# Two decode attentions on one core: B's output weights in other pieces, the last buffers in the free K slot, two result rows

## The chip, the cores and the metric

One core of a Trainium2 chip runs the whole program. The time is the device time of one execution in microseconds (us). Before the change it is 825.41 us, the median of three runs (825.28 to 825.46).

## What is computed

Two attentions, A and B, each of one new token with 32 heads of 128 numbers over a cache of 16384 positions. A uses the whole cache, B only the last 4096 positions. Both results, 512 numbers each, stand side by side in the output.

```
q = x @ wq                                  # [1,512] @ [512,4096], as 32 heads of 128
scores = einsum("bhqd,bhkd->bhqk", q, k) * Dh**-0.5
o = einsum("bhqk,bhkd->bhqd", softmax(scores), v)
out = o.reshape(1, 1, 4096) @ wo            # [1,4096] @ [4096,512]
a: k, v = the whole cache;  b: k, v = cache[:, :, Sk - 4096:, :]
return concatenate([a, b], axis=-1)
```

All inputs are bf16. The caches that are read make 335 MB (268 for A, 67 for B), the four weight matrices 17 MB. Each number of the caches is used once.

## The kernel before

**Tiling.** The work goes in 20 steps (`steps`, `NT`): 16 of A with two heads each, 4 of B with eight heads each; the steps 0, 7, 13 and 19 are B's. Each step has one K tile and one V tile of 8 MB, 128 partitions of 64 KB. K tiles rotate through two slots (`kring`), V tiles through one (`vring`). The weights pass through the V slot too: `wq` of both sides at the start, `wo` of both at the end; the last V tile (`vlast`) goes into a K slot.

**A step.** VectorE multiplies K by q in halves (`scores_prod`, L206) and adds up over the 128 numbers of a head by halving (`scores_tree`, L212, L216). The maximum of each partition (L224) is transposed on TensorE (L228) into a PSUM bank from the pool `ps_m`, taken by head (L234), spread (L238) and transposed back (L241). ScalarE makes the exponentials (L253) and sets them into a masked weight tile `pm` (L260). TensorE multiplies with V (`pv`, L272): 64 matmuls in four column groups of 32 columns each, which write the four quarters of a PSUM bank. `fold` copies that bank to SBUF (`osb`, one buffer with the tag `o4`, L285) and adds the quarters by an fp32 matmul into the side's accumulator (L288).

**The end.** After the last step's maximum (`tile_max`), `normalize`, `own_o` and `spread_o` turn a side's accumulator into `Op`, 128x32 in bf16, one column per row block r of `wo` (L306 to L327). `wo` lies in SBUF as 128 partitions by 32 rows of 512: "row" below is this r, 1 KB per partition, 128 KB in all. A's projection (`project_a`, L336) takes the 32 rows of A in four column groups with 512 columns each, ScalarE copies the result (L341), and a matmul adds the four quarters (`finish_a`, L346). B's projection (`project_b`, L357) cuts every row in four quarters of 128 columns, one per column group; the result stands in four partitions, is cast (L362) and leaves by four output transfers (L364), two from SyncE's queue and two from ScalarE's.

**What sets the order.** The instructions of each engine are in the order of the code (`manual_schedule`). All large loads are issued by SyncE (SP) in order and wait there for a free slot; the 16 DMA engines work their share of each transfer in order of issue. Each load also adds to one of eight counters when it lands. The counters are used in turn, and a load waits until the one before it on its counter has landed. B's `wo` comes in pieces of 16, 8, 4, 3 and 1 rows (`wo_pieces`, `load_wo`, L143) and TensorE waits for each piece where it first reads it.

Of the kernel before, what the change touches and what calls it, by code (L numbers as in the profile page):

```python
# [9 lines left out]
F32 = mybir.dt.float32  # L10
BF16 = mybir.dt.bfloat16
P = 128
# [4 lines left out]
HQ, DH = 32, 128  # L17
# [8 lines left out]
def kernel(  # L26
# [14 lines left out]
    nc = tc.nc  # L41
# [4 lines left out]
    DN = A_wo.shape[1]  # L46
# [5 lines left out]
    kring = ctx.enter_context(tc.tile_pool(name="kring", bufs=2))  # L52
    vring = ctx.enter_context(tc.tile_pool(name="vring", bufs=1))
    small = ctx.enter_context(tc.tile_pool(name="small", bufs=3))
    one = ctx.enter_context(tc.tile_pool(name="one", bufs=1))
    ps_t = ctx.enter_context(tc.tile_pool(name="ps_t", bufs=2, space=bass.MemoryType.PSUM))
    ps_o = ctx.enter_context(tc.tile_pool(name="ps_o", bufs=1, space=bass.MemoryType.PSUM))
    ps_m = ctx.enter_context(tc.tile_pool(name="ps_m", bufs=2, space=bass.MemoryType.PSUM))

    NG = 4  # L60
    QR = P // NG
# [9 lines left out]
    ones = singles.tile([P, 1], F32, tag="ones")  # L71
    fours = singles.tile([P, P], F32, tag="fours")
# [3 lines left out]
    for k, (s, n, x, wq, wo, nh) in enumerate(((A, "A", A_x, A_wq, A_wo, 2), (B, "B", B_x, B_wq, B_wo, 4))):  # L76
# [8 lines left out]
        s.mask = singles.tile([P, nh], F32, tag=f"mask{n}", name=f"mask{n}")  # L85
        s.acc = ps_o.tile([P, 512], F32, tag=f"acc{n}", name=f"acc{n}")
    o_banks = [ps_o.tile([P, 512], F32, tag=f"o{k}", name=f"o{k}") for k in range(2)]

    def by_head(s, ap):
        if s is A:  # L90
# [11 lines left out]
    NT = len(steps)  # L102
# [36 lines left out]
    def load_wo(s, pieces):  # L139
        src = s.wo.rearrange("(p r) f -> p r f", r=HQ)  # L140
        r = 0
        for n in pieces:
            nc.sync.dma_start(out=s.wo_t[:, r : r + n, :], in_=src[:, r : r + n, :])  # L143
            r += n

    def make_masks(s):
# [73 lines left out]
    def tile_max(T):  # L220
        un = tiles[T]
        U = un.s.units
        m = small.tile([P, 2], F32, tag="m", name="m")
        nc.vector.tensor_reduce(  # L224
            out=m[:, 0:U], in_=un.sc[:, :].rearrange("p (u n) -> p u n", u=U), axis=AX.X, op=ALU.max
        )
        un.sm = ps_m.tile([P, P + 2], F32, tag="sm", name="sm")
        nc.tensor.transpose(un.sm[0:U, 0:P], m[:, 0:U], identf[:, :])  # L228

    def max_all(T):  # L230
        un = tiles[T]
        s, U = un.s, un.s.units
        M = small.tile([2, 4], F32, tag="M", name="M")
        nc.vector.tensor_reduce(  # L234
            out=M[0:U, 0 : s.nh], in_=by_head(s, un.sm[0:U, 0:P]), axis=AX.X, op=ALU.max
        )
        Mr = one.tile([2, P], F32, tag="Mr", name="Mr")
        nc.vector.tensor_copy(  # L238
            by_head(s, Mr[0:U, :]), M[0:U, 0 : s.nh].unsqueeze(2).broadcast_to([U, s.nh, P // s.nh])
        )  # L240
        nc.tensor.transpose(un.sm[:, P : P + U], Mr[0:U, :], identf[0:U, 0:U])  # L241
# [38 lines left out]
    def fold(T, u):  # L280
        un = tiles[T]
        s = un.s
        rows = 4 * s.nh
        osb = one.tile([P, 512], F32, tag="o4", name="o4")
        nc.scalar.copy(osb[:, :], un.o[u][:, :])  # L285
        per = QR // rows
        q, off = divmod(s.units * un.g + u, per)
        nc.tensor.matmul(  # L288
            s.acc[QR * q : QR * (q + 1), :], lhsT=s.fold[:, (per - 1 - off) * rows : (per - 1 - off) * rows + QR],
            rhs=osb[:, :], start=(off == 0), stop=(off == per - 1),  # L290
        )

    def square():
        return one.tile([P, P], F32, tag="sq", name="sq")

    def pick_blocks(o, src, n, weight):
        nc.vector.tensor_scalar(out=o, in0=src[:, 0:n], scalar1=weight[:, 0:1], scalar2=None, op0=ALU.mult)
        for j in range(1, 4):
            nc.vector.scalar_tensor_tensor(
                out=o, in0=src[:, j * n : (j + 1) * n], scalar=weight[:, j : j + 1], in1=o, op0=ALU.mult, op1=ALU.add  # L300
            )

    def normalize(s):
        n = HQ // s.nh
        sums = square()
        nc.vector.tensor_tensor(  # L306
            out=sums[:, :].rearrange("p (t h c) -> p t h c", t=n, h=s.nh),
            in0=s.cs[:, :].unsqueeze(2).unsqueeze(3).broadcast_to([P, n, s.nh, 4]),
            in1=s.mask[:, :].unsqueeze(1).unsqueeze(3).broadcast_to([P, n, s.nh, 4]), op=ALU.mult,
        )  # L310
        s.ps = ps_t.tile([P, 1 + P], F32, tag="tp", name="sums")
        nc.tensor.matmul(s.ps[:, 0:1], lhsT=sums[:, :], rhs=ones[:, :], start=True, stop=True)
        s.rq = small.tile([P, 5], F32, tag="rq", name="rq")
        nc.vector.reciprocal(s.rq[:, 4:5], s.ps[:, 0:1])
        nc.vector.tensor_scalar(
            out=s.rq[:, 0:4], in0=quad[:, :], scalar1=s.rq[:, 4:5], scalar2=None, op0=ALU.mult
        )

    def own_o(s):
        s.own = square()  # L320
        pick_blocks(s.own[:, :], s.acc[:, :], DH, quad)

    def spread_o(s):
        nc.tensor.matmul(s.ps[:, 1 : 1 + P], lhsT=fours[:, :], rhs=s.own[:, :], start=True, stop=True)
        t = small.tile([P, HQ], F32, tag="t", name="t", bufs=1)
        pick_blocks(t[:, :], s.ps[:, 1 : 1 + P], HQ, s.rq)
        nc.vector.tensor_copy(s.Op[:, :], t[:, :])  # L327

    def o_column(s, r):
        return s.Op[:, r : r + 1].broadcast_to([P, QR])  # L330

    def project_a():
        ps = ps_t.tile([P, DN], F32, tag="tp", name="wide")
        for r in range(HQ):
            g = r % NG
            nc.tensor.matmul(  # L336
                ps[QR * g : QR * (g + 1), :], lhsT=o_column(A, r), rhs=A.wo_t[:, r, :],
                start=(r < NG), stop=(r >= HQ - NG),
            )
        A.wide = one.tile([P, DN], F32, tag="o4", name="wide_sb")  # L340
        nc.scalar.copy(A.wide[:, :], ps[:, :])  # L341

    def finish_a():
        ps = ps_m.tile([1, DN], F32, tag="sm", name="out_a")
        first = A.fold[:, QR - A.rows : QR - A.rows + 1]
        nc.tensor.matmul(ps[:, :], lhsT=first, rhs=A.wide[:, :], start=True, stop=True)  # L346
        row = one.tile([1, DN], BF16, tag="sc", name="row_a")
        nc.scalar.copy(row[:, :], ps[:, :])
        for f in range(0, DN, DN // 2):
            nc.scalar.dma_start(out=out[0, :, f : f + DN // 2], in_=row[:, f : f + DN // 2])  # L350

    def project_b():
        w = DN // NG
        ps = ps_m.tile([P, w], F32, tag="sm", name="out_b")
        for r in range(HQ):
            for g in range(NG):
                nc.tensor.matmul(  # L357
                    ps[QR * g : QR * (g + 1), :], lhsT=o_column(B, r), rhs=B.wo_t[:, r, g * w : (g + 1) * w],
                    start=(r == 0), stop=(r == HQ - 1),
                )  # L360
        rows = one.tile([P, w], BF16, tag="Mr", name="rows_b")
        nc.vector.tensor_copy(rows[:, :], ps[:, :])  # L362
        for g in range(NG):
            (nc.sync if g % 2 else nc.scalar).dma_start(  # L364
                out=out[0, :, DN + g * w : DN + (g + 1) * w], in_=rows[QR * g : QR * g + 1, :]
            )

    wo_pieces = (16, 8, 4, 3, 1)
    with tc.manual_schedule():
        xrow = one.tile([2, D], BF16, tag="pm", name="xrow")  # L370
        for s in (B, A):
# [36 lines left out]
        for T in range(NT):  # L408
            if T >= 1:
                if T + 1 < NT:  # L410
                    new_k(T + 1)
                    load_k(T + 1)
                else:
                    load_v(T, kslot("vlast"))
            scores_prod(T, 0)
            if T >= 1:
                max_all(T - 1)
                soft(T - 1)
            scores_tree(T, 0)
            if T >= 1:  # L420
                for u in range(tiles[T - 1].s.units):
                    pv(T - 1, u)
                for u in range(tiles[T - 1].s.units):
                    fold(T - 1, u)
            if T + 1 < NT:
                load_v(T, vslot("vt"))
            else:
                wot = vslot("wot")
                for k, s in enumerate((A, B)):
                    s.wo_t = flat(wot[:, k * CH : (k + 1) * CH, :]).rearrange("p (r f) -> p r f", r=HQ)  # L430
                load_wo(A, (HQ,))
                load_wo(B, wo_pieces)
            scores_prod(T, 1)
            scores_tree(T, 1)
            tile_max(T)
        max_all(NT - 1)
        soft(NT - 1)
        normalize(A)
# [1 line left out]
        pv(NT - 1, 0)  # L440
        spread_o(A)
        pv(NT - 1, 1)
        for u in range(2):
            fold(NT - 1, u)
        normalize(B)
        own_o(B)
        project_a()
        spread_o(B)
        finish_a()
        project_b()  # L450


# [28 lines left out]
```

## Time and profile before

| | us |
|---|---|
| median of three runs | 825.41 |
| the profiled execution | 825.65 |
| its span, first to last instruction | 823.9 |
| VectorE busy | 766.4 (93%) |
| TensorE matmuls busy | 184.5 (22%) |
| ScalarE busy | 61.4 (7%) |
| `vlast` issued | 761.25 |
| `wo` of A issued, then B's pieces | 786.96 |
| last piece of B's `wo` issued | 801.1 |
| `OpA` ready | 808.99 |
| first output transfers (A) issued | 817.22 |
| B's cast (L362) begins | 821.14 |

The profile is one execution. The page lists each engine's busy time, a line of digits for 40 slices of the span (9 is a share of 90% or more), and the chain of work that ended last: from the last instruction back, at each step, to what released it. A window gives the busy time in one stretch; its DMA share is the mean over the 16 DMA engines, so 0.25 means four engines' worth of work. The timeline merges like instructions that follow each other, and names in square brackets the idle time ahead of them and what ended it. "SPq" and "ACTq" are the issuing of transfers by SyncE and ScalarE. The trace also records each addition to a counter by a landing transfer; these are called completion records here.

### The profile page before, as it was taken

The numbers are of one execution on the slowest core, as the hardware profiler recorded it, in microseconds if no ns is written. First come the engines' busy times: TensorE is split into PE (matmuls) and PEld (weight loads), VectorE is DVE, ScalarE is ACT, GpSimd is POOL, SyncE is SP. The second block draws the span as 40 slices with busy tenths as digits, with TensorE's granted clock in tenths as the row PEclk, the third lists the DMA queues.
The fourth block names the chain that finished last, engine by engine and source line by source line (L and its number), as shares of the span: only waits on it lengthen the run. The fifth ranks groups of instructions, "written<-read, shape, count | busy, mean of one in ns | idle before, by whom it ended". The sixth has DMA issues, their size and how long they took to land.

```text
span 823.9 us, 3928 instructions
## 1 busy us (share of the span) xinstructions
PE 184.5 (22%) x1606; PEld 60.9 (7%) x1606; DVE 766.4 (93%) x348; ACT 61.4 (7%) x165; POOL 0.7 (0%) x6
## 2 busy tenths in 40 slices
PE   3402312213030303220303112030402030303037
PEld 1100000001010001000000001010100010101012
DVE  2899899999999999999999999999999998999992
ACT  0102000001010000100000001010200000000011
POOL 0000000000000000000000000000000000000000
PEclk9755556565665656555656565555656565656568
DMA  9999999999999999999999999999999999999997
GB/s 384 434 431 435 449 420 449 426 437 433 430 436 430 422 441 439 414 449 427 439 423 443 420 445 413 453 417 428 435 449 420 452 418 442 427 422 441 423 429 292
DMA packets 8097, 352.57 MB, mean 428 GB/s; under 512 B 908, under 2 KB 1040, under 8 KB 1296
## 3 DMA queue, kind: packets, MB, share of 16 engines
q1 hardware_dynamic: 8068, 352.33, 99.2%
q8 instruction: 12, 0.20, 0.1%
q14 instruction: 5, 0.04, 0.0%
q10 hardware_dynamic: 12, 0.00, 0.0%
HBM read 352.32 MB, written 0.00 MB: 428 GB/s over the span
## 4 chain that ended last, share of the span: by engine, by line
DMA 56%; DVE 43%; issue 0%; SPq 0%; PE 0%; DVEq 0%
DMA kt<-in_A_k_cache_dram 44%; DVE kt L206 20%; DVE kt L212 20%; DMA kt<-in_B_k_cache_dram 5%; DMA vlast<-in_B_v_cache_dram 4%; DMA wot<-in_B_wo_dram 4%; DVE sc L216 3%; DVE Mr L238 0%; DVE M L234 0%; SPq L135 0%; SPq L122 0%; PE out_b L357 0%; DVE rows_b L362 0%; DVEq L216 0%
## 5 line engine op out<-in xcount | busy, mean ns | idle before, releaser
L212 DVE TENSOR_TENSOR kt<-kt 128x8192 bf16<-128x8192 bf16 (+3 forms) x160 | 345.0, 2156 | 4.8
L206 DVE TENSOR_TENSOR kt<-kt,qA 128x16384 bf16<-128x16384 bf16 x32 | 278.0, 8687 | 13.2 <-DMA kt<-in_A_k_cache_dram 13.2
L272 PE MATMUL o<-vt,pm 128*8 128x512 bf16 (+1 forms) x1216 | 113.9, 553 | 181.7 <-DMA vt<-in_A_v_cache_dram 161.1
L206 DVE TENSOR_TENSOR kt<-kt,qB 128x16384 bf16<-128x16384 bf16 x8 | 69.5, 8684 | 14.1 <-DMA kt<-in_B_k_cache_dram 14.1
L228 PE MATMUL sm<-identf,m 128*1 128x128 f32 (+1 forms) x20 | 7.4, 371 | 235.2 <-DVE m L224 235.2
L272 PEld LDWEIGHTS <-pm 128*8 128x8 bf16 (+1 forms) x1280 | 39.9, 114 | 253.2 <-issue 206.8
L216 DVE TENSOR_REDUCE sc<-kt 128x128 f32<-128x1024 bf16 x40 | 48.8, 1220 | 2.7
L241 PE MATMUL sm<-identf,Mr 1*128 1x1 f32 (+1 forms) x20 | 5.2, 261 | 178.5 <-DVE Mr L238 178.5
L247 ACT ACTIVATE bias<-sm 128x1 f32<-128x1 f32 (+1 forms) x20 | 3.4, 172 | 447.3 <-PE sm L241 447.3
L285 ACT COPY o<-o 128x512 f32<-128x512 f32 x24 | 14.1, 587 | 264.6 <-PE o L272 233.8
L228 PEld LDWEIGHTS sm<-identf,m 128*1 128x1 f32 (+1 forms) x20 | 1.6, 79 | 252.4 <-issue 241.2
L288 PE MATMUL accA<-o,foldA 128*32 128x512 f32 x32 | 16.7, 605 | 11.1 <-ACT o L285 11.1
L241 PEld LDWEIGHTS sm<-identf,Mr 1*128 1x128 f32 (+1 forms) x20 | 3.5, 176 | 184.9 <-DVE Mr L238 184.9
L260 ACT ACTIVATE pm<-p,maskA 128x256 bf16<-128x256 bf16 x32 | 14.5, 502 | 0.5
L183 PE MATMUL qp<-wqt,xbA 128*128 128x512 bf16 x32 | 9.4, 465 | 10.6 <-DMA wqt<-in_A_wq_dram 10.6
L253 ACT ACTIVATE p<-sc,bias 128x256 bf16<-128x256 f32 (+1 forms) x24 | 11.3, 472 | 0.6
L288 PE MATMUL accB<-o,foldB 128*32 128x512 f32 x16 | 9.9, 709 | 2.7 <-ACT o L285 2.7
L260 ACT ACTIVATE pm<-p,maskB 128x128 bf16<-128x128 bf16 x32 | 10.3, 392 | 0.3
L183 PE MATMUL qp<-wqt,scratch 128*128 128x512 bf16 x32 | 8.9, 447 | 5.0 <-DMA wqt<-in_B_wq_dram 5.0
L224 DVE TENSOR_REDUCE m<-sc 128x1 f32<-128x256 f32 (+1 forms) x20 | 8.4, 420 | 0.7
L272 PE MATMUL o<-vlast,pm 128*16 128x512 bf16 x64 | 6.1, 552 | 1.6 <-ACT pm L260 1.6
L234 DVE TENSOR_REDUCE M<-sm 1x2 f32<-1x128 f32 (+1 forms) x20 | 5.4, 271 | 0.6 <-PE sm L228 0.6
(60 smaller groups left out, 52.9 us busy)
## 6 DMA issues: line engine op xcount, KB each, us to landing
kt<-in_B_k_cache_dram SPq DMA_DIRECT2D x8, 4096.0 KB, 30.0
vt<-in_B_v_cache_dram SPq DMA_DIRECT2D x6, 4096.0 KB
vlast<-in_B_v_cache_dram SPq DMA_DIRECT2D x2, 4096.0 KB, 39.2
wqt<-in_B_wq_dram SPq DMA_DIRECT2D x1, 4096.0 KB, 12.5
wqt<-in_A_wq_dram SPq DMA_DIRECT2D x1, 4096.0 KB
wot<-in_A_wo_dram SPq DMA_DIRECT2D x1, 4096.0 KB
wot<-in_B_wo_dram SPq DMA_DIRECT2D x1, 2048.0 KB
wot<-in_B_wo_dram SPq DMA_DIRECT2D x1, 1024.0 KB
```

The lines of the kernel that those rows point to most:

```text
L183: nc.tensor.matmul(qp[:, :, :], lhsT=s.xb[:, j, c, :], rhs=wq[:, c, j, g : g + 4, :], start=(k == 0), stop=(k == n - 1),)
L206: nc.vector.tensor_tensor(out=k, in0=k, in1=s.q[:, j : j + 1, :].broadcast_to([P, CH, DH]), op=ALU.mult)
L212: nc.vector.tensor_tensor(out=k[:, :, 0:w], in0=k[:, :, 0:w], in1=k[:, :, w : 2 * w], op=ALU.add)
L216: nc.vector.tensor_reduce(out=tiles[T].sc[:, u * CH : (u + 1) * CH], in_=k[:, :, 0:8], axis=AX.X, op=ALU.add)
L224: nc.vector.tensor_reduce(out=m[:, 0:U], in_=un.sc[:, :].rearrange("p (u n) -> p u n", u=U), axis=AX.X, op=ALU.max)
L228: nc.tensor.transpose(un.sm[0:U, 0:P], m[:, 0:U], identf[:, :])
L241: nc.tensor.transpose(un.sm[:, P : P + U], Mr[0:U, :], identf[0:U, 0:U])
L253: nc.scalar.activation(out=un.part(p, u), in_=un.part(un.sc, u), func=ACT.Exp, scale=inv, bias=bias[:, u : u + 1], accum_out=s.cs[:, col + ...
L260: nc.scalar.activation(out=un.pm[u][:, :, j, :], in_=un.part(p, u).rearrange("p (i c) -> p i c", c=4), func=ACT.Copy, scale=s.mask[:, j : ...
L272: nc.tensor.matmul(o[r0 : r0 + rows, :], lhsT=un.pm[u][:, i, :, :].rearrange("p a b -> p (a b)"), rhs=V[T][:, u * un.n + 4 * i : u * un.n ...
L285: nc.scalar.copy(osb[:, :], un.o[u][:, :])
L288: nc.tensor.matmul(s.acc[QR * q : QR * (q + 1), :], lhsT=s.fold[:, (per - 1 - off) * rows : (per - 1 - off) * rows + QR], rhs=osb[:, :], s ...
```

## The change

B's pieces become 8, 8, 3, 8, 4 and 1 rows, and the piece of three rows is split by partitions into 119 and 9. B's first 19 rows are multiplied whole, with 512 columns in four column groups as A's are, copied by VectorE into `s.wide`, and added to the result by a join of two fp32 matmuls (`join_b`). The rows 19 to 31 are cut in two halves of 256 columns and use two column groups. B's result stands in two partitions and leaves by two output transfers, one per queue. The tile `late` (8 buffers of 512 fp32 numbers) takes the K slot that the last K tile leaves: the two last folds, the wide copies of A and B, and the squares of `normalize` and `own_o` have a buffer each, where one `o4` and one `sq` were shared. `normalize(B)` moves ahead of the last folds. Two fixed PSUM banks (`sm_banks`) take the place of the pool `ps_m`.

```diff
-    ps_m = ctx.enter_context(tc.tile_pool(name="ps_m", bufs=2, space=bass.MemoryType.PSUM))
+    sm_banks = [ps_o.tile([P, 512], F32, tag=f"sm{k}", name=f"sm{k}") for k in range(2)]
...
-        for n in pieces:
-            nc.sync.dma_start(out=s.wo_t[:, r : r + n, :], in_=src[:, r : r + n, :])
+        for n, cuts in pieces:
+            for a, b in zip((0,) + cuts, cuts + (P,)):
+                nc.sync.dma_start(out=s.wo_t[a:b, r : r + n, :], in_=src[a:b, r : r + n, :])
             r += n
...
-        un.sm = ps_m.tile([P, P + 2], F32, tag="sm", name="sm")
+        un.sm = sm_banks[T % 2]
...
-        osb = one.tile([P, 512], F32, tag="o4", name="o4")
+        osb = late[:, u, :] if T == NT - 1 else one.tile([P, 512], F32, tag="o4", name="o4")
...
-        sums = square()
+        sums = late[:, 4 + s.k, 0:P]
...
-        s.own = square()
-        pick_blocks(s.own[:, :], s.acc[:, :], DH, quad)
+        s.own = late[:, 6 + s.k, 0:DH]
+        pick_blocks(s.own, s.acc[:, :], DH, quad)
...
-    def project_a():
+    def wide_rows(s, n):
         ps = ps_t.tile([P, DN], F32, tag="tp", name="wide")
-        for r in range(HQ):
+        for r in range(n):
             g = r % NG
             nc.tensor.matmul(
-                ps[QR * g : QR * (g + 1), :], lhsT=o_column(A, r), rhs=A.wo_t[:, r, :],
-                start=(r < NG), stop=(r >= HQ - NG),
+                ps[QR * g : QR * (g + 1), :], lhsT=o_column(s, r), rhs=s.wo_t[:, r, :],
+                start=(r < NG), stop=(r >= n - NG),
             )
-        A.wide = one.tile([P, DN], F32, tag="o4", name="wide_sb")
-        nc.scalar.copy(A.wide[:, :], ps[:, :])
+        s.wide = late[:, 2 + s.k, :]
+        if s is A:
+            nc.scalar.copy(s.wide, ps[:, :])
+        else:
+            nc.vector.tensor_copy(s.wide, ps[:, :])
...
-    def project_b():
-        w = DN // NG
-        ps = ps_m.tile([P, w], F32, tag="sm", name="out_b")
-        for r in range(HQ):
-            for g in range(NG):
+    def tail_b(r0, r1, wide):
+        w = DN // 2
+        for r in range(r0, r1):
+            for g in range(2):
                 nc.tensor.matmul(
-                    ps[QR * g : QR * (g + 1), :], lhsT=o_column(B, r), rhs=B.wo_t[:, r, g * w : (g + 1) * w],
-                    start=(r == 0), stop=(r == HQ - 1),
+                    sm_banks[1][QR * g : QR * (g + 1), 0:w], lhsT=o_column(B, r),
+                    rhs=B.wo_t[:, r, g * w : (g + 1) * w], start=(r == wide), stop=(r == HQ - 1),
                 )
+    def join_b():
+        w = DN // 2
+        for g in range(2):
+            nc.tensor.matmul(
+                sm_banks[1][QR * g : QR * (g + 1), 0:w], lhsT=first.broadcast_to([P, QR]),
+                rhs=B.wide[:, g * w : (g + 1) * w], start=False, stop=False,
+            )
+    def store_b():
+        w = DN // 2
+        rows = one.tile([2 * QR, w], BF16, tag="Mr", name="rows_b")
+        nc.vector.tensor_copy(rows[:, :], sm_banks[1][0 : 2 * QR, 0:w])
+        for g, queue in enumerate((nc.sync, nc.scalar)):
+            queue.dma_start(out=out[0, :, DN + g * w : DN + (g + 1) * w], in_=rows[QR * g : QR * g + 1, :])
...
-    wo_pieces = (16, 8, 4, 3, 1)
+    wo_pieces = ((8, ()), (8, ()), (3, (119,)), (8, ()), (4, ()), (1, ()))
+    wide_n = 19
...
+        late = kring.tile([P, 8, 512], F32, tag="kring", name="late")
         max_all(NT - 1)
         soft(NT - 1)
         normalize(A)
...
         pv(NT - 1, 1)
+        normalize(B)
         for u in range(2):
             fold(NT - 1, u)
-        normalize(B)
         own_o(B)
-        project_a()
+        wide_rows(A, HQ)
         spread_o(B)
         finish_a()
-        project_b()
+        wide_rows(B, wide_n)
+        tail_b(wide_n, 27, wide_n)
+        join_b()
+        tail_b(27, HQ, wide_n)
+        store_b()
```

More of the change, by code (lines that the diff above doesn't have):

```diff
@@ L291, in fold @@
         )
-    def square():
-        return one.tile([P, P], F32, tag="sq", name="sq")
     def pick_blocks(o, src, n, weight):
@@ L304, in normalize @@
         n = HQ // s.nh
-        sums = square()
+        sums = late[:, 4 + s.k, 0:P]
         nc.vector.tensor_tensor(
-            out=sums[:, :].rearrange("p (t h c) -> p t h c", t=n, h=s.nh),
+            out=sums.rearrange("p (t h c) -> p t h c", t=n, h=s.nh),
             in0=s.cs[:, :].unsqueeze(2).unsqueeze(3).broadcast_to([P, n, s.nh, 4]),
@@ L311, in normalize @@
         s.ps = ps_t.tile([P, 1 + P], F32, tag="tp", name="sums")
-        nc.tensor.matmul(s.ps[:, 0:1], lhsT=sums[:, :], rhs=ones[:, :], start=True, stop=True)
+        nc.tensor.matmul(s.ps[:, 0:1], lhsT=sums, rhs=ones[:, :], start=True, stop=True)
         s.rq = small.tile([P, 5], F32, tag="rq", name="rq")
@@ L319, in own_o @@
     def own_o(s):
-        s.own = square()
-        pick_blocks(s.own[:, :], s.acc[:, :], DH, quad)
+        s.own = late[:, 6 + s.k, 0:DH]
+        pick_blocks(s.own, s.acc[:, :], DH, quad)
     def spread_o(s):
-        nc.tensor.matmul(s.ps[:, 1 : 1 + P], lhsT=fours[:, :], rhs=s.own[:, :], start=True, stop=True)
+        nc.tensor.matmul(s.ps[:, 1 : 1 + P], lhsT=fours[:, :], rhs=s.own, start=True, stop=True)
         t = small.tile([P, HQ], F32, tag="t", name="t", bufs=1)
@@ L343, in finish_a @@
+    first = A.fold[:, QR - A.rows : QR - A.rows + 1]
     def finish_a():
-        ps = ps_m.tile([1, DN], F32, tag="sm", name="out_a")
-        first = A.fold[:, QR - A.rows : QR - A.rows + 1]
-        nc.tensor.matmul(ps[:, :], lhsT=first, rhs=A.wide[:, :], start=True, stop=True)
+        ps = sm_banks[0]
+        nc.tensor.matmul(ps[0:1, :], lhsT=first, rhs=A.wide, start=True, stop=True)
         row = one.tile([1, DN], BF16, tag="sc", name="row_a")
-        nc.scalar.copy(row[:, :], ps[:, :])
+        nc.scalar.copy(row[:, :], ps[0:1, :])
@@ L349, in finish_a @@
         for f in range(0, DN, DN // 2):
             nc.scalar.dma_start(out=out[0, :, f : f + DN // 2], in_=row[:, f : f + DN // 2])
-    def project_b():
-        w = DN // NG
-        ps = ps_m.tile([P, w], F32, tag="sm", name="out_b")
-        for r in range(HQ):
-            for g in range(NG):
+    def tail_b(r0, r1, wide):
+        w = DN // 2
+        for r in range(r0, r1):
+            for g in range(2):
                 nc.tensor.matmul(
-                    ps[QR * g : QR * (g + 1), :], lhsT=o_column(B, r), rhs=B.wo_t[:, r, g * w : (g + 1) * w],
-                    start=(r == 0), stop=(r == HQ - 1),
-                )
[L361 to L365, printed above, removed]
-            )
@@ L430 @@
                     s.wo_t = flat(wot[:, k * CH : (k + 1) * CH, :]).rearrange("p (r f) -> p r f", r=HQ)
-                load_wo(A, (HQ,))
+                load_wo(A, ((HQ, ()),))
                 load_wo(B, wo_pieces)
```

## The prediction

> **What bounds the kernel now.** I read the page first. The DMA row is full in 39 of 40 slices and the chain that ended last is DMA and VectorE in turn, so the input transfers (352 MB at 428 GB/s) set the time; VectorE's 93% lies beside them.
>
> ```profile
> span 823.9 us, 3928 instructions
> DMA  9999999999999999999999999999999999999997
> DMA 56%; DVE 43%; issue 0%; SPq 0%; PE 0%; DVEq 0%
> ```
>
> The change leaves the bytes and the twenty steps alone, so only the end can move. I read the chain of waits there (start, length, what):
>
> ```profile
> 791.37 29.14 DMA wot<-in_B_wo_dram
> 820.51 0.04 issue
> 820.55 0.56 PE out_b L357 x16
> 821.14 0.29 DVE rows_b L362
> ```
>
> B's `wo` ends the chain at 820.51, and what follows is short: matmuls, a cast, the output. Then the last microseconds in windows of 0.25 us (window, length, busy time of PE, PEld, DVE, ACT, POOL with counts, granted clock, DMA share of 16 engines, GB/s):
>
> ```profile
> 817.00:817.25 0.25, 0.25 (x32) 0.25 (x24) 0.00 (x0) 0.19 (x1) 0.00 (x0) 1.00 0.61 238
> ...
> 818.25:818.50 0.25, 0.24 (x18) 0.24 (x21) 0.00 (x0) 0.00 (x0) 0.00 (x0) 1.00 0.24 90
> ...
> 819.00:819.25 0.25, 0.00 (x0) 0.00 (x0) 0.00 (x0) 0.00 (x0) 0.00 (x0) 1.00 0.25 98
> ```
>
> The DMA share falls in steps: 0.61 and later 0.24, that is about nine and then four of 16 engines. The engines don't end together. The trace's completion records say it sharply; each transfer of 128 partitions leaves 16, one per engine. For the last row of `wo` they stand in three groups: seven **early** engines at 817.08 to 817.76, five at 818.62 to 818.94, four **late** ones at 820.20 to 820.81. A's `wo` ended in the same groups 10 us before (last 810.80), so the lag is old. It grows through the run where an instruction fetch (page: queue q8, 12 packets of 16 KB) takes an engine's time: the transfer landing at 80.3 us, just after the fetch at 78.3, shows one engine 1.9 us behind the other fifteen. The last transfer could end near the mean of its 16 records, 818.6, if the work were shared by lag.
>
> Last, the timeline of the end (start, length, engine, line):
>
> ```profile
> 810.98 0.59 ACT L285 COPY o<-o 128x512 f32<-128x512 f32 x1 [3.44 <-PE accB L288]
> 811.62 1.04 PE L288 MATMUL accB<-o,foldB 128*32 128x512 f32 x2 [0.68 <-ACT o L285]
> 812.91 1.91 PE L336 MATMUL wide<-wot,OpA 128*32 128x512 bf16 x32
> 816.58 0.18 DVE L327 CAST OpB<-t 128x32 bf16<-128x32 f32 x1
> 816.82 1.08 PE L357 MATMUL out_b<-wot,OpB 128*32 128x128 bf16 x64 [0.24 <-DVE OpB L327]
> 818.26 0.63 PE L357 MATMUL out_b<-wot,OpB 128*32 128x128 bf16 x32 [0.36 <-DMA wot<-in_B_wo_dram]
> 821.14 0.29 DVE L362 CAST rows_b<-out_b 128x128 bf16<-128x128 f32 x1 [4.37 <-PE out_b L357]
> 821.46 0.62 SPq L364 DMA_DIRECT2D out_dram<-rows_b  x2
> ```
>
> The second fold waits 3.44 us for the single `o4` buffer; PE works off each piece of B's `wo` as it lands.
>
> **1. Three rows through 119 and 9 partitions.** In every traced transfer the engines have equal shares: 128 partitions give 16 completions, the `xrow` and output rows one packet on one engine. 119 is 7 times 17, so equal shares mean seven engines with 17 rows of 3 KB; nine give nine engines one row. Which seven no row shows. The nearest sign: the packet of the first `row_a` transfer, a one-engine transfer, starts at 817.94 without a gap in any of the nine streams still running, so it ran on an engine that had ended, an early one. I take it that small counts start from the same end of the engines and that the seven are the early seven. A 3 KB row costs 0.124 us (three rows before: an early engine's completions 815.75 and 816.74, 8 packets in 0.99). The early seven get 18 rows for 8, +1.24: they end at 819.00 at the latest. The others lose 8 (two of them 7), 8 of them being 1.04 on a late engine (819.47 to 820.51): the last ends at 819.8 to 819.9, **0.9 us earlier**. Bounds: no gain, or +1.24 if a late engine is among the seven.
>
> [...]
>
> SP issues `wo` as A, 8, 8, 3 (two issues, 0.42 us each), 8, 4, 1 rows. The built program makes the later three wait for a counter: the third 8 for the last `vlast` (801.09), the 4 for A's `wo` (810.80), the 1 for the first 8 (about 813.3). Behind them stands only SP's output issue. Early engines come to these pieces at about 814.2, 816.6 and 817.9, 2 us or more after their issue, so no engine runs dry; cost zero, 1 us if it did.
>
> **2. B's first 19 rows whole.** 19 matmuls of 512 columns take the place of 76 of 128. From L336 (32 in 1.91 us, 0.38 for one): 0.38 + 18 x 0.049 = 1.3 us. `OpB` was ready at 816.76. Now the second fold does not wait for the buffer: ACT copies it at 810.1 instead of 810.98, both folds run back to back, `own_o(B)` ends near 813.9 instead of 814.86, and `OpB` comes at about 816.1, behind `wide_rows(A)`. So the 19 rows end by 817.4 (818.0 without that gain). VectorE's new copy of 128x512: the cast of 128x128 took 0.29, ACT's copy of 128x512 0.59, VectorE's slope between 32 and 128 columns (L299, 0.251 and 0.351) gives 0.69; done by 818.1, or 818.7. The join needs it at 819.1. Cost nothing; without that cover, the excess.
>
> **3. Rows 19 to 31 in two column groups, and the join.** The third 8 lands where row 23 landed before, 818.22 (late engines carry nothing of the three rows). 16 matmuls of 256 columns: before, 64 of 128 in four groups began 0.0134 us apart; half the groups and twice the columns make 0.053 apart, so streams end near 819.15. The join: two fp32 matmuls; L288's of 512 columns has two passes 0.42 us apart, so 0.21 here; overlapped 0.6, one after the other 0.85. Then rows 27 to 30, 0.43 us (their piece landed at 819.47, hidden), row 31 with 0.11, and 0.17 for the last to leave (0.22 for 128 columns less 0.05 streaming). PE ends at 820.45 to 820.75; I take **820.5**, 0.6 before the 821.11 of now. The last row's landing (819.9) is no longer what ends last: PE is. If two groups don't overlap, all doubles: 16 x 0.107 + 1.05 + 10 x 0.107 + 0.17 = 4.0 us, ending at 822.3.
>
> **4. Two result rows.** The cast is 64x256: 0.29 + 128 columns at 1.04 ns = 0.42, **+0.13** (0 to +0.4). One output per queue: the completion records are 822.50 and 822.69 for the first of each queue, 822.87 and 823.04 for the second, so the end comes **0.35 earlier**. The 0.86 us from there to the span's end stays.
>
> **5. Fixed max banks, `late`.** `late` sits in the slot of the last K tile, which VectorE itself freed at 799.3. ACT's first copy into it gains four waits on DMA counters, for K loads long landed; ACT was idle 2.00 us before that copy. Nothing. The max banks alternate as the pool's two did. Nothing.
>
> **The sum:** -0.6 + 0.13 - 0.35 = -0.8 us. The profiled execution took 825.65 (span 823.9 and 1.75 around it): 824.85. It lies 0.24 above the median of 825.41, so the median comes to **824.6**, 0.1% lower. A measurement of this kernel tells about 0.2% from no change, so that counts as the same.
>
> **Rivals.**
> - *No relief.* The two pieces spread over all engines as 128 rows did (at most a row more or less each). Landing 820.81, then 0.28 to PE's end as now, +0.13 and -0.35: **825.2**. For it: one engine per 8 partitions is what all large transfers show. [...] Chance 0.07.
> - *Wrong engines.* A late one is among the seven: 820.81 + 1.24 = 822.05, behind it 0.33 of PE, and the rest: +1.0 us, **826.4**. Against it the idle engine of the `row_a` packet. 0.07.
> - *PE's end doubles* (groups one after another, or granted clock 0.50 instead of the windows' 1.00): PE 822.3, +1.2 + 0.13 - 0.35: **826.4**. Against it L336 and L357, where four groups overlap. 0.08.
> - *One engine (the slower side).* If 119 does not divide and goes through one engine, that queue has 119 + 1 - 8 rows more, 112 x 0.124 = 13.9 us, and the last rows stand behind them: 817.1 + 13.9 = 831.0 instead of 820.8, about **835.5**. It decides once one engine has over 30 rows more (3.7 us, its distance to the last). For it: no transfer of a count like 119 is in the trace. 0.03.
>
> The forecast (824.0 to 825.0, from PE at the landing to the join in series) has 0.75. Range: with "no relief" and the lower part of the longer PE end, 824.0 to 825.7. Faster by over 0.2% (below 823.8) would need more than all terms: 0.05. Same 0.87. Slower (above 827.1): one engine, or two of the milder rivals together, 0.08.
>
> **What would show it.** Right: windows near 819 with a DMA share well above 0.25 and zero from 820; PE's last matmul at 820.5 behind the join and not behind a DMA; ACT's second fold copy without its 3.44; a cast of 0.42. Wrong: an idle PE before row 31 (the landing still ends last), a wait for the three-row piece, or any difference before 787 us, where the programs are the same.

## The result and the profile after

The changed kernel takes 830.68 us (median of 4 runs, 830.47 to 831.2) against 825.43 us: a ratio of 1.0065, 95% interval 1.005 to 1.008. It is **slower by 5.25 us**, where 824.6 was forecast. The profiled execution took 831.2 us with a span of 829.1, so 2.1 us lie around the span instead of 1.75.

The page of the kernel after: the same stages in the same shares, the DMA row full to the end.

```profile
span 829.1 us, 3757 instructions
DMA  9999999999999999999999999999999999999995
DMA 56%; DVE 43%; PE 0%; issue 0%; SPq 0%; DVEq 0%
```

The end of the chain of waits after (start, length, what):

```profile
800.58 22.12 DMA wot<-in_B_wo_dram
822.70 0.04 issue
822.74 1.89 PE sm L358 x16
824.63 0.85 PE sm L366 x4
825.49 1.08 PE sm L358 x10
826.57 0.02 issue
826.59 0.42 DVE rows_b L374
```

As forecast, TensorE with the join in it ends the chain, not the last row. But the third 8 lands at 822.70 instead of 818.22, and what follows takes 3.83 us instead of 2.25. Windows of 1 us say when it goes wrong (last three columns: granted clock, DMA share, GB/s):

```profile
811.00:812.00 1.00, 1.00 (x24) 0.57 (x20) 0.93 (x3) 0.00 (x0) 0.00 (x0) 1.00 1.01 418
812.00:813.00 1.00, 1.00 (x12) 0.40 (x3) 0.44 (x2) 0.31 (x1) 0.00 (x0) 1.00 1.04 301
814.00:815.00 1.00, 0.86 (x9) 0.22 (x9) 0.40 (x2) 0.58 (x1) 0.00 (x0) 1.00 0.95 212
816.00:817.00 1.00, 0.00 (x0) 0.00 (x0) 0.00 (x0) 0.00 (x0) 0.00 (x0) 1.00 0.95 259
817.00:818.00 1.00, 0.74 (x8) 0.13 (x7) 0.00 (x0) 0.00 (x0) 0.00 (x0) 0.50 1.03 268
```

Two things stand here side by side. From 812 on the 16 DMA engines are all busy (share about 1), and yet only 212 to 303 GB/s arrive up to 818 instead of 418: the same packets take longer. And from 817 on the granted clock is 0.50. The timeline after shows the waits ahead of that:

```profile
814.25 0.18 DVE L325 CAST OpB<-t 128x32 bf16<-128x32 f32 x1
814.49 0.62 PE L334 MATMUL wide<-wot,OpB 128*32 128x512 bf16 x8
817.26 1.04 PE L334 MATMUL wide<-wot,OpB 128*32 128x512 bf16 x8 [2.15 <-DMA wot<-in_B_wo_dram]
820.54 0.61 PE L334 MATMUL wide<-wot,OpB 128*32 128x512 bf16 x3 [2.24 <-DMA wot<-in_B_wo_dram]
821.20 0.69 DVE L342 COPY late<-wide 128x512 f32<-128x512 f32 x1 [6.76 <-PE wide L334]
822.74 1.89 PE L358 MATMUL sm<-wot,OpB 128*32 128x256 bf16 x16 [1.59 <-DMA wot<-in_B_wo_dram]
```

TensorE waits three times for pieces of `wo`, 1.6 to 2.2 us each, and after the first of these waits eight matmuls take 1.04 us that took 0.62 before it.

The completion records carry no engine's number, but their spacing tells the groups. The piece over 119 partitions leaves seven records: 815.28 to 816.98 (four), 818.38, 820.07 and 820.29. The one over 9 leaves nine. The records of A's `wo` and of the second 8 just before form the same three groups as in the kernel before, so the seven are read as four early engines, one of the middle group and two late ones. From 812 to 818 most 3 KB packets took 0.15 to 0.25 us and most 8 KB packets 0.43 to 0.58 (medians 0.207 and 0.482), against 0.125 and 0.313 in the median before.

**The theories.** *T*: cutting a transfer by partitions makes the engines slow each other, and the waits that follow cost clock. Rivals: *shares* (119 deals rows to late engines, the prediction's "wrong engines"); *pieces* (more and smaller transfers); *the other edits* (buffers, order, column groups, join).

### The profile page after: what moved, and what is told of

Same layout as the page of the kernel before. It is cut to its first block, busy times and chain, and to the rows that moved or that the text cites. A ratio compares the mean times of both kernels' runs of the same rounds, so it can differ in the third digit from the quotient of the medians.

```text
span 829.1 us, 3757 instructions
## 1 busy us (share of the span) xinstructions
PE 182.9 (22%) x1527; PEld 61.0 (7%) x1527; DVE 767.3 (93%) x349; ACT 61.5 (7%) x165; POOL 0.7 (0%) x6
## 4 chain that ended last, share of the span: by engine, by line
DMA 56%; DVE 43%; PE 0%; issue 0%; SPq 0%; DVEq 0%
DMA kt<-in_A_k_cache_dram 43%; DVE kt L207 20%; DVE kt L213 20%; DMA kt<-in_B_k_cache_dram 5%; DMA vlast<-in_B_v_cache_dram 5%; DVE sc L217 3%; DMA wot<-in_B_wo_dram 3%; PE sm L358 0%; DVE Mr L239 0%; DVE M L235 0%; SPq L135 0%; PE sm L366 0%; SPq L122 0%; DVE m L225 0%; DVE rows_b L374 0%
## 5 line engine op out<-in xcount | busy, mean ns | idle before, releaser
L273 PE MATMUL o<-vt,pm 128*8 128x512 bf16 (+1 forms) x1216 | 110.2, 539 | 182.0 <-DMA vt<-in_A_v_cache_dram 161.3
L289 PE MATMUL accB<-o,foldB 128*32 128x512 f32 x12 | 7.6, 721 | 2.0 <-ACT o L286 2.0
```

The source lines that it names most:

```text
L273: nc.tensor.matmul(o[r0 : r0 + rows, :], lhsT=un.pm[u][:, i, :, :].rearrange("p a b -> p (a b)"), rhs=V[T][:, u * un.n + 4 * i : u * un.n ...
L289: nc.tensor.matmul(s.acc[QR * q : QR * (q + 1), :], lhsT=s.fold[:, (per - 1 - off) * rows : (per - 1 - off) * rows + QR], rhs=osb[:, :], s ...
```

## The experiments

All medians stand beside the kernel before on the same chip, 825.31 to 825.39 us in every batch.

### One part alone, one part undone

`e1_uncut` is the kernel after without the cut; `e2_cut_only` the kernel before with the cut pieces, which `load_wo` takes as in after, and nothing else.

```diff
 e1, from after:
-    wo_pieces = ((8, ()), (8, ()), (3, (119,)), (8, ()), (4, ()), (1, ()))
+    wo_pieces = ((8, ()), (8, ()), (3, ()), (8, ()), (4, ()), (1, ()))
 e2, from before:
-    wo_pieces = (16, 8, 4, 3, 1)
+    wo_pieces = ((8, ()), (8, ()), (3, (119,)), (8, ()), (4, ()), (1, ()))
```

> The changed kernel with the three rows in one transfer of 128 partitions. Theory T (the cut sets it: it puts work on late engines and slows the other engines' packets): the last row lands near 820.8 us of the span as before, bandwidth stays above 400 GB/s until 816, and the median falls from 830.7 to 826.0 (clock 1.00 at the end) or 827.7 (0.50). Rival R (B's tail in two column groups with the join sets it): the median stays above 829. Rival Q (the order 8, 8, 3, 8, 4, 1 with its later issues starves engines): stays above 829, with DMA share falling below 0.9 before 816.

> The kernel before, with only B's wo pieces changed to 8, 8, 119 and 9 partitions of three, 8, 4, 1. T: the last row lands near 824.3 as in the changed kernel; the four-group tail follows in 0.3 us, so the median is about 829.0, 3.5 above the kernel before. R: about 825.4, as before. Q: about 829 too, so it is e1 that tells T from Q.

Measured: e1 827.06 us (ratio 1.0016, 1.0007 to 1.0025), e2 828.78 us (1.0041, 1.0026 to 1.0056). Undoing the cut wins 3.6 us, the cut alone costs 3.5: nearly additive. e2 lies 0.2 us from what T had, e1 between the two values that T gave for the two clocks; R's and Q's values for e1, above 829, did not come. In e1 over 390 GB/s arrive until 816; in e2, whose matmuls and buffers are those of before, the fall is back:

```profile
812.00:813.00 1.00, 1.00 (x28) 0.46 (x20) 0.93 (x4) 0.00 (x0) 0.00 (x0) 1.00 0.97 286
814.00:815.00 1.00, 0.84 (x4) 0.09 (x2) 0.74 (x3) 0.26 (x1) 0.00 (x0) 1.00 1.14 255
816.00:817.00 1.00, 0.20 (x16) 0.07 (x5) 0.00 (x0) 0.00 (x0) 0.00 (x0) 1.00 1.00 266
```

That rules out the other edits for these 3.5 us, of which some 0.2 are a slower tail: e2's granted clock is 0.50 from 820.57 on, and from its last landing to TensorE's end are 0.79 us, 0.60 in the kernel before. It leaves 1.7 us that e1 still loses. Its ten times form two groups, 825.4 to 825.8 and 826.6 to 827.6, and its profile (chain of waits) has the sixteen matmuls at half clock again, after a wait of 2.10 us for the third 8:

```profile
788.33 30.61 DMA wot<-in_B_wo_dram
818.94 0.04 issue
818.99 1.89 PE sm L358 x16
```

### The clock

`e4_warm` is after, `e5_uncut_warm` is e1, each with matmuls that nothing reads in the waits for `wo`.

```diff
+    def warm(n):
+        for i in range(n):
+            g = i % NG
+            nc.tensor.matmul(o_banks[0][QR * g : QR * (g + 1), :], lhsT=o_column(A, i % HQ),
+                             rhs=A.wo_t[:, i % HQ, :], start=True, stop=True)
...
+        warm(36)        # ahead of tail_b; e4 also 40 behind the rows 7 and 15
         tail_b(wide_n, 27, wide_n)
```

> The changed kernel with 40, 40 and 36 added matmuls of 512 columns into an unused bank in the three places where TensorE waits for B's wo. They change no result. T (TensorE's clock falls to 0.50 because it idles 2 us at a time, and two groups overlap well): clock 1.00 to the end, 16 matmuls of 256 columns in 1.1 us instead of 1.89, TensorE ends 0.3 us behind the last landing, the median 1.7 lower, 829.0. If two groups don't overlap: 1.89 stays, the median 830.7.

> e1_uncut with 36 added matmuls of 512 columns into an unused bank between B's 19 wide rows and the third piece of 8 (where TensorE waited 2.10 us). They change no result. Theory (e1's slower runs are those in which TensorE's clock falls to 0.50 in that wait): clock 1.00 to the end, 16 matmuls in 1.1 us, all runs together within 0.4 us, median 825.0 to 825.2. If the clock isn't what spreads e1's runs: median 826 to 827 and the spread of 2 us stays.

Measured: e4 829.14 us (1.0045, 1.0029 to 1.0062), 1.5 below after; e5 825.72 us (1.0004, 0.9995 to 1.0014), 1.3 below e1, and its ten times span 0.28 us instead of 2.1. In e5's windows the clock is 1.00 until 823, so the two groups of e1 are read as the clock. At full clock the tail is what the prediction said it would be (timeline of e4):

```profile
822.46 1.05 PE L368 MATMUL sm<-wot,OpB 128*32 128x256 bf16 x16
823.33 0.61 PE L376 MATMUL sm<-late,foldA 128*32 128x256 f32 x4
823.77 0.73 PE L368 MATMUL sm<-wot,OpB 128*32 128x256 bf16 x10
```

From 822.46 to the cast are 2.05 us, against the 2.25 worked out. So the two column groups do overlap; the doubling (sixteen matmuls in 1.89 us at clock 0.50, in 1.05 at 1.00) came from the clock alone. e5's expected time was 0.5 us too low: it left out 0.3 us around the span (below).

### Shares or cut

Three other cuts of the three rows. The shares are an estimate, worked out as equal ones from the 16, seven and nine records that transfers over 128, 119 and 9 partitions leave in the kernels before and after: at 112 every engine gets seven rows and then one, at 64 four and four; 120 and 8 are eights, as 128 rows on 16 engines are.

```diff
-    wo_pieces = ((8, ()), (8, ()), (3, (119,)), (8, ()), (4, ()), (1, ()))
+    wo_pieces = ((8, ()), (8, ()), (3, (112,)), (8, ()), (4, ()), (1, ()))   # e3; e7: 64, e8: 120
```

> The changed kernel with the three rows cut at 112 partitions instead of 119, so that 16 engines have 7 rows and then 1 row each: equal shares, but rows of other engines' partitions. If unequal shares alone do it: as e1_uncut within 0.4 us. If engines that write to other engines' partitions slow each other: packets of 3 KB take 0.2 us as in the changed kernel, bandwidth falls below 350 GB/s for some microseconds, and the median is 1 us or more above e1_uncut.

> The changed kernel cut at 64 instead of 119 partitions: two transfers of 64, equal shares of 4 + 4 rows. If any cut moves rows to other engines than the ones that serve these partitions in the 128-partition transfers, and this slows both: bandwidth falls below 350 GB/s as with 112, median 1 us or more above e1_uncut (827.1). If half the rows stay with their engine, the loss is smaller than with 112 (829.8): 828. If only a count that 16 doesn't divide evenly into eights hurts: as e1_uncut.

> The changed kernel cut at 120 and 8: 15 engines with 8 rows, then 8 engines with one row. If in a 128-partition transfer each engine serves 8 partitions in a row, nearly all rows stay with their engine: no fall of bandwidth before 816, median 826 to 828 like e1_uncut. If the assignment of 128 partitions is another one (scattered), the rows are other engines': bandwidth below 350 GB/s for some microseconds and a median of 829 to 830 as with 112.

Measured: e3 829.81 us (1.0052, 1.0037 to 1.0067), e7 830.53 us (1.0063, 1.0048 to 1.0078), e8 829.64 us (1.0054, 1.0037 to 1.007), with 256 to 290 GB/s from 812 to 816 in all three. Equal shares save at most 1.0 of the 3.6 us that the cut costs; if the shares are those worked out, most of it has nothing to do with who carries how much. e7's case that half of the rows stay undisturbed (828) missed. e8's first case, eight partitions in a row to an engine in an uncut transfer too, missed, and its second came: the fall is there. Which partitions an engine serves, no run shows.

### Pieces, bytes and addresses

`e9_cut_cols` sends the three rows as two uncut transfers of two rows and one. `e10_more_whole` adds 384 KB that nothing reads, from one stretch of DRAM, uncut, into a tile `late` that has 16 buffers from here to e14; `e11_more_cut` cuts that load alone, at 119.

```diff
 e9, from e5:
-    wo_pieces = ((8, ()), (8, ()), (3, ()), (8, ()), (4, ()), (1, ()))
+    wo_pieces = ((8, ()), (8, ()), (2, ()), (1, ()), (8, ()), (4, ()), (1, ()))
 e10, from e5, behind the 19 rows:
+        more = late[:, 8:10, :].rearrange("p a b -> p (a b)")[:, 0:768].bitcast(BF16)
+        spare = B_k_cache[0, 0, 0 : 12 * P, :].rearrange("(p l) d -> p (l d)", p=P)
+        for a, b in ((0, P),):          # e11: ((0, 119), (119, P))
+            nc.sync.dma_start(out=more[a:b, :], in_=spare[a:b, :])
```

> e5_uncut_warm with the three rows of B's wo as two transfers again, but of 2 rows and 1 row, each over all 128 partitions, so the partitions are not cut. Theory (a cut by partitions makes all engines slow each other; the number and size of the pieces cost nothing): as e5_uncut_warm, 825.7 us, at most 0.3 more, and over 390 GB/s in every microsecond from 811 to 816. Rival (one more and smaller transfer in the row of pieces is what slows): 828 to 829 us, with 260 to 300 GB/s from about 812.

> e5_uncut_warm with one more load of 384 KB that nothing reads (a piece of B's K cache outside the window, read in one stretch of DRAM, into a free part of the tile late), over all 128 partitions, between the three rows and the third 8. All theories: 393,216 bytes at 428 GB/s are 0.92 us, so 826.6 us, and over 390 GB/s from 811 to 817. It is the measure for e11_more_cut.

> e10_more_whole with the extra load cut at partition 119, as two transfers of 119 and 9 partitions; wo itself is not cut. Theory (which engines carry which partitions of SBUF is what slows, whatever is loaded): 2.5 to 3.5 us above e10_more_whole, about 829.6 us, with 250 to 300 GB/s for some 8 us from about 812 on. Rival (the slow part is in DRAM: wo's rows are 1 KB pieces 32 KB apart, and a cut deals their addresses to the engines in another way): as e10_more_whole, within 0.4 us, since here the source is one stretch.

Measured: e9 825.67 us (1.0004, 0.9994 to 1.0013), as e5; e10 826.8 us (1.0017, 1.0008 to 1.0027); e11 829.87 us (1.0054, 1.0039 to 1.0069), 3.1 above e10. One more piece costs nothing, and 384 KB uncut cost 1.1 us. The same 384 KB cut cost 3.1 us more although `wo` itself is whole there and the source is one stretch, so these 3.1 us need neither a cut `wo` nor its addresses in DRAM. Windows, first of e10, then of e11:

```profile
814.00:815.00 1.00, 0.86 (x10) 0.22 (x9) 0.51 (x3) 0.47 (x1) 0.00 (x0) 1.00 1.03 414
816.00:817.00 1.00, 0.66 (x13) 0.40 (x16) 0.22 (x1) 0.00 (x0) 0.00 (x0) 1.00 1.04 422
```

```profile
814.00:815.00 1.00, 0.95 (x2) 0.09 (x2) 0.86 (x5) 0.00 (x1) 0.00 (x0) 1.00 1.08 262
816.00:817.00 1.00, 0.37 (x8) 0.21 (x8) 0.00 (x0) 0.00 (x0) 0.00 (x0) 1.00 1.10 267
```

### What the engines share

`e13_own_half` and `e14_other_half` send 384 KB as four transfers of eight partitions, every fourth one; only the first partition differs.

```diff
 from e10:
-        more = late[:, 8:10, :].rearrange("p a b -> p (a b)")[:, 0:768].bitcast(BF16)
-        spare = B_k_cache[0, 0, 0 : 12 * P, :].rearrange("(p l) d -> p (l d)", p=P)
-        for a, b in ((0, P),):
-            nc.sync.dma_start(out=more[a:b, :], in_=spare[a:b, :])
+        more = late[:, 8:14, :].rearrange("p a b -> p (a b)").bitcast(BF16)
+        spare = B_k_cache[0, 0, 0 : 48 * 32, :].rearrange("(t e l) d -> t e (l d)", t=4, e=8)
+        for t in range(4):
+            nc.sync.dma_start(out=more[0 + t : 0 + 32 : 4, :], in_=spare[t, :, :])
                                     # e14:   more[64 + t : 64 + 32 : 4, :]
```

> e5_uncut_warm with the 384 KB of e10_more_whole loaded another way: four transfers of 8 partitions with 12 KB each, the partitions t, t+4, ... t+28 for t = 0 to 3. [...] From rows of this case: 12 KB are one and a half 8 KB packets of 0.31 us, so 4 x 0.46 = 1.9 us more on eight engines; where a late engine is among them, as with the seven of 119, the end comes at most 1.9 us later: 826.5 to 827.6 us. [...]

> e13_own_half with the four transfers aimed at the partitions 64 + t to 92 + t, and nothing else changed: same bytes, same source, same number of engines, same shares. [...] Rival (any cut transfer is slow, or none of such a small number of partitions is): within 0.4 us of e13_own_half.

Measured: e13 840.6 us (1.0184, 1.0169 to 1.0199), e14 845.42 us (1.0241, 1.0225 to 1.0256). Both totals are far above the 826.5 to 827.6 us that were worked out for e13, by a fault of mine in both: VectorE's write into another part of `late` waited for these loads, and everything behind it came late. The timeline of e13 shows the wait:

```profile
817.97 0.29 DVE L303 TENSOR_TENSOR late<-csA,maskA 128x128 f32<-128x128 f32 x1 [17.25 <-DMA late<-in_B_k_cache_dram]
```

So the totals say nothing of the question, but the transfers do: SP had issued everything but the last three pieces of `wo` before 810, and those wait for counters only. Windows of e13, then of e14:

```profile
814.00:815.00 1.00, 0.00 (x0) 0.00 (x0) 0.00 (x0) 0.00 (x0) 0.00 (x0) 0.50 1.09 449
816.00:817.00 1.00, 0.00 (x0) 0.00 (x0) 0.00 (x0) 0.00 (x0) 0.00 (x0) 0.50 1.01 414
```

```profile
814.00:815.00 1.00, 0.00 (x0) 0.00 (x0) 0.00 (x0) 0.00 (x0) 0.00 (x0) 0.50 0.99 201
816.00:817.00 1.00, 0.00 (x0) 0.00 (x0) 0.00 (x0) 0.00 (x0) 0.00 (x0) 0.50 1.05 231
```

Each of the four transfers leaves eight completion records in both kernels. The packets that start from 814 to 816 took, in the median:

| packet | e13 | e14 |
|---|---|---|
| 12 KB (the added loads) | 0.468 us | 0.918 us |
| 8 KB (pieces of `wo`) | 0.313 us | 0.628 us |

The last row of `wo` landed at 821.99 in e13 and 826.36 in e14. Same bytes, same source, same count of completion records: with the loads sent to the partitions 0 to 31, the 8 KB packets of `wo` keep the 0.313 us that they took before, and 391 to 449 GB/s arrive in each microsecond from 814 to 817; with the loads sent to 64 to 95, the packets take twice as long, `wo`'s too (the shortest 8 KB packet of e14 there took 0.586 us, the longest of e13 0.327), and 201 to 231 GB/s arrive. Only the partitions that are written differ between the two runs, so the slowing goes with the place in SBUF; what is shared there, no run shows. That transfers over some of the partitions can slow the packets of the others, as T has it, is shown for these loads, and "any cut transfer is slow" falls. That the cut of `wo` slows in this same way is a reading: no run cuts `wo` itself without a fall.

### What is left around the span

`e6_two_rows` is after with the pieces 16, 8, 4, 3 and 1 and all 32 rows in two column groups, without wide rows and join. `e12_rows_alone` is before with two column groups and two result rows; `e15_banks` and `e16_late` add one edit each to e12: the fixed max banks, or the tile `late`.

```diff
 e12, from before:
-        w = DN // NG
+        w = DN // 2
...
-            for g in range(NG):
+            for g in range(2):
...
-        rows = one.tile([P, w], BF16, tag="Mr", name="rows_b")
-        nc.vector.tensor_copy(rows[:, :], ps[:, :])
-        for g in range(NG):
+        rows = one.tile([2 * QR, w], BF16, tag="Mr", name="rows_b")
+        nc.vector.tensor_copy(rows[:, :], ps[0 : 2 * QR, :])
+        for g in range(2):
```

> The changed kernel with B's pieces as before (16, 8, 4, 3, 1, uncut) and all 32 rows in two column groups, without the 19 wide rows and the join: what is left of the change is the buffers, the earlier normalize of B and the two result rows. If these parts are worth what the prediction gave them: last landing 820.8, TensorE ends 821.1, the cast +0.13, one output less per queue -0.35, median 825.1 to 825.2, 0.2 below the kernel before. If two groups are slower than four: later than before by up to 1 us.

> before with one edit alone: B's projection takes all 32 rows in two column groups of 256 columns, and the result leaves in two rows, one output per queue; pieces, buffers, max banks and the order of normalize are those of before. By the prediction's step 4: the cast 0.42 us for 0.29, the last completion 0.35 earlier, the last matmuls some 0.2 later, so the span is 0.1 to 0.3 us shorter than before's. If the 0.2 to 0.3 us more around the span in all variants of the changed kernel belong to the tile late, the max banks or the order, the time around the span stays at 1.75 to 1.85 here and the time is 825.1 to 825.3; if they belong to the two result rows, it is 2.0 to 2.1 and the time 825.4 to 825.6.

> e12_rows_alone with the two fixed max banks in place of the pool ps_m, and nothing else. If the time around the span (1.81 us in e12_rows_alone, 1.96 in e6_two_rows, 2.12 in all variants with wide rows) grows with the banks, it is 1.9 to 2.0 here and the time 825.4; otherwise 1.81 and 825.3.

> e12_rows_alone with the tile late in the free K slot for the last folds, squares and A's wide copy, and nothing else (normalize of B stays behind the folds). If the time around the span grows with this tile, it is 1.9 to 2.0 here and the time 825.4; otherwise 1.81. In the span, the second fold's 3.44 us wait for the buffer goes, OpB comes earlier, and the end stays where it was, since B's wo lands last.

| | median us | ratio (interval) | around the span, us |
|---|---|---|---|
| before | 825.31 to 825.39 | | 1.8 |
| e2_cut_only | 828.78 | 1.0041 (1.0026 to 1.0056) | 1.79 |
| e12_rows_alone | 825.27 | 0.9998 (0.9989 to 1.0007) | 1.81 |
| e15_banks | 825.22 | 0.9997 (0.9988 to 1.0007) | 1.80 |
| e16_late | 825.6 | 1.0003 (0.9994 to 1.0012) | 1.94 |
| e6_two_rows | 825.53 | 1.0002 (0.9993 to 1.0011) | 1.96 |
| e5_uncut_warm | 825.72 | 1.0004 (0.9995 to 1.0014) | 2.13 |

The last column is a median of ten times (four for e2), and a kernel's single values spread over 0.15 to 0.25 us. The tile `late` brings 0.13 to 0.15, the wide rows of B with their join another 0.17, result rows and max banks nothing. The added matmuls of e5 and the new pieces are not what brings the 0.17: e1, without such matmuls, has 2.12, and e2, with the pieces alone, 1.79. e12 and e15 came as expected; e6 came 0.35 us above the 825.1 to 825.2 that it was given, and e16 0.2 above its 825.4. What happens in this time the trace doesn't show, so why stays open. The best of these, e15, can't be told from before.

## Why the prediction was wrong

**Step 1 failed twice.** It took "that the seven are the early seven" from one idle engine under one output packet; four early, one middle and two late engines it was, as their records are read above. That is the rival "wrong engines", priced at +1.24 us on the landing. The greater failure is one that no rival had: the step charged each engine for its own rows at the undisturbed 0.124 us each and let the others run free. Instead the packets of all pieces grew: from 812 to 818 to 0.207 us for 3 KB and 0.482 for 8 KB in after, from 0.125 and 0.313 before, and in e14 to twice their time in e13. That a cut deals the partitions to other engines than an uncut transfer does, and that engines then slow each other, is my reading of these runs; no record shows which engine wrote where. The third 8, forecast at 818.22, landed at 822.70. Of these 4.48 us, 0.72 are the three rows that were not taken off the late engines (818.94 in e1), 3.76 the cut. In e3, with equal shares by the working above, it landed at 821.26: so by that working 2.3 of the 3.76 are there without any engine carrying more than another, and 1.4 go with the uneven shares (0.9 by the medians of the two kernels), near the price of "wrong engines".

The rival "no relief" was right that cutting a transfer wins nothing, but not by its mechanism: the two pieces did not spread over all engines, as seven and nine records show, and its price of 0 was the error. e7, the cut into halves, took 3.5 us more than e1, while e9's two uncut transfers cost nothing (825.67 us beside e5's 825.72).

**Step 1's "no engine runs dry" held** in its letter, as the DMA share of about 1 until 818 shows, but a full share was not full speed.

**Step 2 erred on its cover.** The 19 rows ended at 821.15, not 817.4, because their pieces came late, not for a lack of TensorE time; `OpB` came at 814.4 rather than 816.1, so its part of the gain was larger than forecast, and worth nothing. The copy took the 0.69 us that were worked out. One of the prediction's signs of being wrong, a wait for the three-row piece, came here: 2.24 us ahead of the last three rows.

**Step 3's working held, its clock did not.** The tail takes 2.05 us at clock 1.00 (e4) against 2.25 worked out, and 3.83 at 0.50. The rival "PE's end doubles" named the granted clock, and its 4.0 us from the landing to TensorE's end is what came (3.87), but I set its chance by the 1.00 of the windows before, where TensorE's waits for pieces were 0.36 to 0.63 us. The change itself made the waits of about 2 us; in e1's trace, without the cut, one wait of 2.10 us stands ahead of the half clock, and seven of its ten times lie in the slower group.

**Step 4 was right in size**: the cast took 0.42 us, and from TensorE's end to the span's end are 2.53 us, 0.07 less than forecast. The sum's carrying over of 1.75 us around the span was wrong by 0.35.

**Step 5** named a cost of nothing for `late`; in the span that held, around it it costs 0.13 to 0.15 us.

In the profiled executions, 831.2 against 824.85 forecast: 4.48 (the third 8's landing) + 1.59 (landing to TensorE's end, 3.87 for 2.28) - 0.07 + 0.35 = 6.35 us. By the medians: the cut 3.4 (e4 above e5, both at clock 1.00), the clock 1.5 (after above e4), and 0.4 for e5 above before, nearly all of it around the span; together 5.3, where 5.25 were measured.

## What to carry to other kernels

Before you deal a transfer out differently, price what that may do to all the other packets, not only which engine carries which rows: here the same 384 KB cost 3.1 us more when cut at partition 119 (e11 above e10), and a DMA share of about 1 with 212 to 303 GB/s instead of 418 was the sign of it (after, 812 to 818). An edit that makes TensorE wait for data has to be priced at half clock for what follows too, unless other matmuls fill the wait: sixteen matmuls took 1.89 us behind waits of 1.6 to 2.1 us (after, e1, e3, e7, e8) and 1.05 where added matmuls filled them (e4, e5). And a small gain at the end needs the time around the span in its sum: 0.3 us there ate the 0.35 that the two outputs saved.

## What was not expected of the hardware

- Transfers of only eight partitions, with eight completion records each, beside uncut pieces: to partitions 64 to 95 they go with packets of twice the time (12 KB 0.918 us, 8 KB 0.628), to partitions 0 to 31 not (12 KB 0.468 us, 8 KB 0.313, as before).
- Every cut of `wo` tried (119, 112, 64 and 120) brought the core from some 400 to 420 GB/s in the microsecond before to 197 to 314 in each microsecond from 812 to 818.
- The stretches of one granted clock. From 784 us on, the full ones last 6.83, 17.07 and 13.65 us in the trace of before, and 6.83, 13.65, 10.24, 10.24 and 3.41 in that of after: each a whole multiple of the shortest to within 0.02 us. In e1 the one at 0.50 from 818.58 on lasts 3.4. In after the clock fell to 0.50 at 817.00, 1.9 us into a wait of 2.15, in e1 1.7 us into one of 2.10; it was back at 1.00 3.0 us (e1) and 6.2 us (e14) after TensorE had work without waits again.
- No single length of a wait decides: e11's clock fell at 818.40 behind two waits of 0.80 and 0.95 us, e10's stayed at 1.00 over one of 1.12. Where a wait falls among such stretches may be what makes e1's two groups; with one trace of e1 that is not shown. With 36 to 40 added matmuls in each wait the clock stayed at 1.00 in e4.
